# Spreading the rows of w2 unevenly over partitions in a decode kernel

## The chip, the cores and the metric

The kernel runs on one core of one Trainium2 chip. The metric is device time in microseconds, from the start of the launch to its end. A profiled execution gives, beside its own time, a span: the stretch from the first to the last recorded instruction.

The engines are written as in the profile: PE multiplies matrices (PEld loads its weights), DVE and ACT work on vectors, POOL runs the set-up and a few small steps, and SP issues nearly all transfers. Transfers run on 16 DMA engines. The profile's times in "us" count from the start of the span.

## The reference

The computation is one decode step: a layer norm, then an attention block over a cache of 65,536 positions in 4 groups of heads, and beside it a mixing MLP; both are added to the input. Cut to what matters:

```python
xn = layernorm(x)                                  # x: 1 x 1 x 1024
# A: attention; 32 query heads share 4 key/value heads, 65536 x 128 each, bf16
q = xn_A @ wq;  p = softmax(q k^T / sqrt(128));  A = (p v) @ wo
# B: mixer
h  = gelu(layernorm(xn) @ w1)                      # w1: 1024 x 1024
hs = concatenate([shift(h[part], step) for four parts]) @ w2   # w2: 1024 x 1024
x1 = xn + hs
B  = x1 + gelu(layernorm(x1) @ w3) @ w4            # w3: 1024 x 3584, w4: 3584 x 1024
out = x + A + B                                    # A takes layernorm(x) as its input
```

The four shifts move `h` along the sequence and pad with zeros. The sequence has one position here, so every shifted part is zero: the vector that multiplies `w2` is all zeros. The kernel holds it as `g_bf`, set to zero by POOL at the start, and still loads `w2` and multiplies with it.

## The kernel before

One large buffer `KV` has three slots of 64 KB on each of the 128 partitions. Everything large passes through it, in this order of issue on SP: `wq` (8 MB, slot 0), `w1` and `w2` (2 MB each, slot 1), `w3` (7 MB, slot 2); then eight pairs of an 8 MB block of keys and an 8 MB block of values, the keys alternately in slots 0 and 2 and the values always in slot 1; then `wo` (8 MB, slot 0) and `w4` in four pieces of 17, 7, 3 and 1 rows per partition (slot 2). Every one of these puts the same number of bytes on every partition. A matrix of R rows lies as R/128 whole rows on each partition (`rows_src`, line 292).

The order of the work is written out by hand. `_op`, `_grp` and `_dma` (lines 117 to 144) record instructions, each with the buffers that it reads and writes, into a list per engine, and a wait is added where another engine has to be done first. SP issues in its order and stops at a wait; so a transfer whose slot is still in use also holds up all that stand behind it. `issue(i)` (line 307) is the load of the i-th key or value block into its slot.

The set-up runs in this order:

- POOL makes constants (lines 315 to 337). It also works inside `layer_norm` (line 355).
- DVE and PE norm `x`, then PE multiplies with `wq` (line 379). When that is done SP may issue the first block of keys into slot 0 (line 384).
- The queries are spread into `Yall` (line 395); a second layer norm follows; then `proj` (line 404) multiplies with `w1`, `gelu` follows, and `proj` multiplies with `w2`. `proj` takes one matrix row per partition at a time: for each of `KT_D` = 8 rows it issues `nt` matmuls of 512 columns (line 411), 2 for `w1` and `w2`, 7 for `w3`; DVE copies the sums (line 419) and PE transposes them (line 426).
- When the matmuls with `w2` are done, SP may issue the first block of values into slot 1 (line 446). A third layer norm, `proj` with `w3` and `gelu` follow, and then SP waits for all engines and issues the second block of keys into slot 2 (lines 450 and 451).

Then comes a loop over the eight blocks (line 594). DVE transposes the keys in place in four pieces (`Ttr`, line 460), PE makes the scores (`QK`, line 474), DVE and ACT the softmax (lines 481 to 502), PE and DVE transpose the weights (lines 505 and 509), and PE multiplies with the values (`PV`, line 518). At the end of a block SP may issue the values of the next block, and behind these the keys of the one after it (lines 633 and 637). In the last block the four pieces of `w4` are issued after the last scores (line 557). At the end PE multiplies with `wo` (line 578) and, as the pieces arrive, with `w4` (line 566); DVE copies the result and SP stores it (lines 647 and 648).

Of the kernel before, what the change touches and what calls it, by code (L numbers as in the profile page):

```python
# [6 lines left out]
BF = mybir.dt.bfloat16  # L7
# [92 lines left out]
def _deps(q, reads, writes):  # L100
    evs = [e for b in reads for e in b.w.items()]
    for b in writes:
        evs += list(b.w.items()) + list(b.r.items())
    q.wait_all(evs, in_order=q.name == "pe")


def _done(ev, reads, writes, partial=False):
    for b in reads:
        b.add_read(ev)
    for b in writes:  # L110
        if partial:
            b.add_write(ev)
        else:
            b.set_write(ev)


def _op(q, fn, reads=(), writes=(), partial=False, loop=False):
    _deps(q, reads, writes)
    ev = q.op(fn, True, loop)
    _done(ev, reads, writes, partial)  # L120
    return ev


def _grp(q, fns, reads=(), writes=(), partial=False):
    _deps(q, reads, writes)
    ev = None
    for i, fn in enumerate(fns):
        ev = q.op(fn, i == len(fns) - 1)
    _done(ev, reads, writes, partial)
    return ev  # L130
# [8 lines left out]
def _dma(q, chan, fn, reads=(), writes=(), partial=False):  # L139
    _deps(q, reads, writes)  # L140
    chan.n += 1
    ev = q.dma(fn, chan.sem, 16 * chan.n)
    _done(ev, reads, writes, partial)
    return ev


def bass_parallel_sum__gqa_block_cached__mixer_s_mlp__decode_kernel(
# [13 lines left out]
    P = 128  # L161
    D = A_x.shape[2]
# [5 lines left out]
    KT_D = D // P  # L168
# [3 lines left out]
    NBLK = HKV * SK // BLK  # L172
    BPH = SK // BLK
    SLOT = BLK * DH // P
    assert DH == P and G == 8 and HKV == 4 and D == 1024 and HQD == 4096 and F == 3584 and SK == 2 * BLK
    SCALE = float(DH) ** -0.5
    EPS = 1e-5

    with ExitStack() as es:
        E = es.enter_context  # L180

        def sb(name, shape, dt):
            return E(nc.sbuf_tensor(name, shape, dt))
# [4 lines left out]
        def sem(name):  # L188
            return E(nc.semaphore(name))
# [25 lines left out]
        sb("pad", [P, pad // 4], F32)  # L215
        KV = sb("KV", [P, 3, SLOT], BF)
        cb_rL = sb("cb_rL", [P, 1], F32)
# [7 lines left out]
        def early(n, dt):  # L225
            size = n * (2 if dt is F32 else 1)
            o = e_off[0]
            e_off[0] = o + (size + 15) // 16 * 16
            assert e_off[0] <= SLOT
            v = KV[:, 2, o:o + size]  # L230
            return v.bitcast(F32) if dt is F32 else v
# [20 lines left out]
        ln_xc = early(KT_D, F32)  # L252
        ln_sq = early(KT_D, F32)
        qT_bf = early(HQ, BF)
        g_bf = early(KT_D, BF)
        h1g_bf = early(KT_D, BF)
        ge_x = early(KT_F, F32)
        ge_a = early(KT_F, F32)
# [11 lines left out]
        q_pool = _Q("pool", sem("c_pool"))  # L270
        q_sp = _Q("sp", None)
        chans = {}

        def chan(name):
            if name not in chans:
                chans[name] = _DmaChan(sem("d_" + name))
            return chans[name]

        b_const = _B()
# [9 lines left out]
        def kv_load(s, ch, src, n, bufs=None):  # L289
            _dma(q_sp, chan(ch), lambda e: e.dma_start(out=KV[:, s, 0:n], in_=src), writes=b_KV[s] if bufs is None else bufs)  # L290

        def rows_src(w, r0, nrow):
            return w.rearrange("(p r) n -> p (r n)", p=P)[:, r0 * w.shape[1]:(r0 + nrow) * w.shape[1]]
# [3 lines left out]
        b_w1 = b_KV[1][0:2]  # L297
        b_w2 = b_KV[1][2:4]
        kv_load(1, "w1", rows_src(B_w1, 0, 8), 8 * D, b_w1)
        _dma(q_sp, chan("w2"), lambda e: e.dma_start(out=KV[:, 1, 8 * D:16 * D], in_=rows_src(B_w2, 0, 8)), writes=b_w2)  # L300
        kv_load(2, "s2", rows_src(B_w3, 0, 8), 8 * F)

        def slot(i):
            m, isv = divmod(i - 3, 2)
            return 1 if isv else 2 * (m % 2)

        def issue(i):
            if i < 3 + 2 * NBLK:
# [3 lines left out]
                src = cache[0, h, nb * BLK:(nb + 1) * BLK, :].rearrange("(p c) d -> p (c d)", p=P)  # L312
                kv_load(slot(i), "v" if isv else "s%d" % slot(i), src, SLOT)

# [6 lines left out]
        def sel(t_, pattern, op, base, mult, fill):  # L321
            return q_pool.op(lambda e: e.affine_select(out=t_, in_=t_, pattern=pattern, compare_op=op, fill=fill, base=base, channel_multiplier=mult))
# [12 lines left out]
        q_pool.wait_all([ev])  # L335
        ev = sel(maskA, [[32, 4], [0, 8]], ALU.is_ge, 31, -1, 0.0)
        b_const.set_write(ev)

        _op(q_dve, lambda e: e.tensor_copy(xT, x_bf), reads=[b_x], writes=[b_xT])  # L339

        def layer_norm(src, b_src, dst_f, dst_bf, b_dst, c0):
# [27 lines left out]
            reads=[b_M, b_misc], writes=[b_misc])  # L369
# [6 lines left out]
        for j in range(KT_D):  # L376
            for b in range(2):
                for jj in range(4):
# [3 lines left out]
                        start=(j == 0), stop=(j == KT_D - 1), tile_position=(0, 32 * jj)))  # L382
# [5 lines left out]
                                                 start=(b + i == 0), stop=True, skip_group_check=True)  # L388
# [4 lines left out]
        for h in range(HKV):  # L393
            for we in range(4):
# [3 lines left out]
                    reads=[b_M, b_const], writes=[b_Y], partial=(h + we > 0))  # L398
# [2 lines left out]

        kvstep = KV[:].ap[0][0]

        def proj(s, o, ncol, vec, bank, reads, c0):
            nper = ncol // P
            nt = nper // 4
            fns = []
            for j in range(KT_D):
                for k in range(nt):
                    mv = bass.AP(KV[:].tensor, s * SLOT + o + j * ncol + 4 * k, [[kvstep, P], [nper, P], [1, 4]])  # L410
                    fns.append(lambda e, j=j, k=k, mv=mv: e.matmul(  # L411
                        S_ps[32 * (k % 4):32 * (k % 4) + 32, bank + k // 4, :], vec[:, j:j + 1].broadcast_to([P, 32]), mv,
                        start=(j == 0), stop=(j == KT_D - 1), tile_position=(0, 32 * (k % 4))))
            nbank = (nt + 3) // 4
            _grp(q_pe, fns, reads=reads, writes=b_S[bank:bank + nbank])
            for b in range(nbank):
                nb = min(4, nt - 4 * b)
                if b == 0:
                    _op(q_dve, lambda e, b=b, nb=nb: e.tensor_copy(pT_f[0:32 * nb, b, :], S_ps[0:32 * nb, bank + b, :]), reads=[b_S[bank + b]], writes=[b_pT[b]])  # L419
                else:  # L420
                    _op(q_act, lambda e, b=b, nb=nb: e.activation(pT_f[0:32 * nb, b, :], S_ps[0:32 * nb, bank + b, :], ACTF.Copy), reads=[b_S[bank + b]], writes=[b_pT[b]])
            fns = []
            for b in range(nbank):
                nb = min(4, nt - 4 * b)
                for c in range(4):
                    fns.append(lambda e, b=b, nb=nb, c=c: e.matmul(  # L426
                        M_ps[:, c0 + 16 * b + c:c0 + 16 * b + 4 * nb:4], pT_f[0:32 * nb, b, c:512:4], ident_f[0:32 * nb, 0:32 * nb:32],
                        start=(b + c == 0), stop=True, skip_group_check=True))
            _grp(q_pe, fns, reads=b_pT[0:nbank] + [b_const], writes=[b_M])

        def gelu(src_ps, width, dst_bf, b_src, b_dst):
# [7 lines left out]
            _op(q_dve, lambda e: e.tensor_tensor(out=dst_bf, in0=a_, in1=xs_, op=ALU.mult), reads=[b_misc], writes=[b_dst])  # L439

        proj(1, 0, D, xn2_bf, 2, b_w1 + [b_xn2], 256)
        gelu(M_ps[:, 256:256 + KT_D], KT_D, h1g_bf, b_M, b_h1)
        proj(1, 8 * D, D, g_bf, 3, b_w2 + [b_const], 272)
        _op(q_dve, lambda e: e.tensor_tensor(out=x1, in0=xn, in1=M_ps[:, 272:272 + KT_D], op=ALU.add), reads=[b_xn, b_M], writes=[b_x1])
        _op(q_dve, lambda e: e.tensor_tensor(out=acc[:], in0=acc[:], in1=M_ps[:, 272:272 + KT_D], op=ALU.add), reads=[b_acc, b_M], writes=[b_acc])
        issue(4)
        layer_norm(x1, b_x1, xn3, xn3_bf, b_xn3, 208)
        proj(2, 0, F, xn3_bf, 0, b_KV[2] + [b_xn3], 288)
        gelu(M_ps[:, 288:288 + KT_F], KT_F, gh_bf[:], b_M, b_gh)
        q_sp.wait_all([(q.sem, q.cnt) for q in (q_pe, q_dve, q_act, q_pool)])  # L450
# [15 lines left out]
        def QK(n):  # L466
# [3 lines left out]
            for we in range(4):  # L470
                w_hi, e_ = divmod(we, 2)
                for cm in range(4):
                    mv = bass.AP(KV[:].tensor, s * SLOT + sub * 8192 + cm * 128 + w_hi * 64 + e_, [[kvstep, P], [512, 16], [2, 32]])
                    fns.append(lambda e, we=we, cm=cm, mv=mv: e.matmul(  # L474
# [119 lines left out]
        for m in range(NBLK):  # L594
            n = 4 * m
# [38 lines left out]
            if m == NBLK - 2:  # L634
                kv_load(0, "wo", A_wo.rearrange("(p r) n -> p (r n)", p=P), SLOT)
            else:
# [93 lines left out]
```

## Time and profile before

| | |
|---|---|
| median of 5 runs | 400.4 us (400.31 to 400.64) |
| profiled execution, its time | 400.39 us |
| its span | 399.1 us |
| bytes read | 169.87 MB |
| busy: DVE | 221.3 us |
| busy: PE | 176.2 us |
| busy: PE weight loads | 60.6 us |
| busy: ACT | 23.9 us |
| busy: POOL | 7.6 us |
| 16 DMA engines, main queue | 98.7% of the span |

The busy times are of engines that work beside each other. The share of the DMA engines is a mean over the 16 of them. Beside instructions the trace keeps two kinds of records of transfers. One is the packets: start, duration and size of each piece that a DMA engine moved, but not the engine's number. The other is the landing marks: the times at which the 16 DMA engines reported their parts of a transfer done, 16 for each transfer.

### The profile page before, as it was taken

The page shows a single profiled execution, that of the slowest core. Times are in us where ns is not written, and L with a number is a line of the kernel's source. Part 1 is how long each engine was busy: PE and PEld are TensorE (multiplying, and loading weights), DVE is VectorE, ACT ScalarE, POOL GpSimd, SP SyncE. Part 2 cuts the span into 40 slices and gives each one's busy share as a digit, 9 for nine tenths or more (in the row PEclk, how much of TensorE's full clock was granted, in tenths as well). Part 3 has the DMA queues.
Part 4 walks back from the last instruction along what each step waited for, and adds up shares of the span by engine and source line. Part 5 has one row for each costly group of instructions (what it writes and reads, how often), then busy time and mean ns, then how long its engine had stood idle before and what let it go on. Part 6 is the DMA issues. An engine that isn't in the chain of part 4 may idle for free.

```text
span 399.1 us, 3500 instructions
## 1 busy us (share of the span) xinstructions
PE 176.2 (44%) x1539; PEld 60.6 (15%) x1539; DVE 221.3 (55%) x260; ACT 23.9 (6%) x50; POOL 7.6 (2%) x31
## 2 busy tenths in 40 slices
PE   0034768148034713570357036413651462147394
PEld 0022335012001200120012011100120110012232
DVE  0024221995298549834984597269647952896200
ACT  1000000011001100110011002000100110011000
POOL 5000000000000000000000000000000000000000
PEclk9998656556755765565558555855585558556979
DMA  9999899999999999999999999999999999999995
GB/s 421 421 388 493 383 434 480 435 420 427 416 440 420 420 461 453 420 427 420 440 427 420 447 466 420 421 420 427 440 427 447 466 420 420 420 427 440 416 414 229
DMA packets 3759, 169.97 MB, mean 426 GB/s; under 512 B 548, under 2 KB 552, under 8 KB 808
## 3 DMA queue, kind: packets, MB, share of 16 engines
q1 hardware_dynamic: 3608, 169.87, 98.7%
q8 instruction: 5, 0.08, 0.1%
q10 hardware_dynamic: 144, 0.00, 0.0%
q14 instruction: 2, 0.02, 0.0%
HBM read 169.87 MB, written 0.00 MB: 426 GB/s over the span
## 4 chain that ended last, share of the span: by engine, by line
DMA 58%; DVE 25%; PE 13%; issue 1%; ACT 1%; SPq 1%; POOL 0%
DMA KV<-in_A_k_cache_dram 45%; DVE KV L460 18%; DMA KV<-in_B_w_dram 8%; DMA KV<-in_A_x_dram 6%; PE S_ps L411 3%; PE OT_ps L518 2%; DVE mrow L481 2%; PE M_ps L426 2%; PE S_ps L474 2%; PE S_ps L379 2%; ACT p_sb L496 1%; DVE Yall L395 1%; DVE pT_f L509 1%; PE PT_ps L505 1%; DVE pT_f L419 1%
## 5 line engine op out<-in xcount | busy, mean ns | idle before, releaser
L460 DVE STREAM_TRANSPOSE KV<-KV 128x4096 f32<-128x4096 f32 x32 | 140.3, 4421 | 43.3 <-DMA KV<-in_A_k_cache_dram 43.3
L474 PE MATMUL S_ps<-KV,Ycur 128*32 128x512 bf16 x512 | 60.7, 623 | 127.2 <-DVE KV L460 127.2
L518 PE MATMUL OT_ps<-KV,pT_f 128*32 128x512 bf16 x512 | 46.3, 501 | 1.2 <-DVE pT_f L509 1.2
L474 PEld LDWEIGHTS S_ps<-KV,Ycur 128*32 128x32 bf16 x512 | 14.3, 126 | 158.9 <-DVE KV L460 141.4
L496 ACT ACTIVATE p_sb<-S_ps,brun 128x1024 bf16<-128x1024 f32 x16 | 17.8, 1113 | 275.1 <-DVE brun L494 174.7
L509 DVE STREAM_TRANSPOSE pT_f<-PT_ps 128x512 f32<-128x512 f32 x32 | 22.5, 702 | 14.0 <-PE PT_ps L505 14.0
L481 DVE TENSOR_REDUCE mrow<-S_ps 128x1 f32<-128x1024 f32 x16 | 19.3, 1205 | 11.3 <-PE S_ps L474 11.3
L484 PE MATMUL M_ps<-Rm,Lmat 128*128 128x16 bf16 x16 | 3.1, 194 | 38.0 <-DVE Rm L482 38.0
L505 PE MATMUL PT_ps<-p_sb,permR 128*128 128x512 bf16 x32 | 18.4, 576 | 0.8
L529 DVE SCALAR_TENSOR_TENSOR O_acc<-O_acc,ff,OT_ps 128x512 f32<-128x512 f32 x12 | 9.0, 748 | 13.9 <-PE OT_ps L518 13.9
L518 PEld LDWEIGHTS OT_ps<-KV,pT_f 128*32 128x32 bf16 x512 | 12.8, 114 | 23.6 <-issue 15.3
L411 PE MATMUL S_ps<-KV 128*32 128x512 bf16 x88 | 12.6, 564 | 2.7 <-DVE KV L359 2.7
L339 DVE CAST KV<-KV 128x8 f32<-128x8 bf16 x1 | 0.2, 172 | 22.1 <-DMA KV<-in_A_x_dram 22.1
L578 PE MATMUL S_ps<-KV,o_bf 128*1 128x512 bf16 x64 | 9.3, 463 | 5.1 <-DMA KV<-in_A_wo_dram 5.1
L484 PEld LDWEIGHTS M_ps<-Rm,Lmat 128*128 128x128 bf16 x16 | 1.7, 104 | 49.3 <-DVE Rm L482 49.3
L426 PE MATMUL M_ps<-ident_f,pT_f 64*128 64x2 f32 (+2 forms) x32 | 7.9, 372 | 2.4 <-DVE pT_f L419 2.4
L582 DVE COPY pT_f<-S_ps 1x512 f32<-1x512 f32 x1 | 0.7, 680 | 14.4 <-PE S_ps L578 14.4
L426 PEld LDWEIGHTS M_ps<-ident_f,pT_f 64*128 64x128 f32 (+2 forms) x32 | 7.7, 326 | 4.7 <-DVE pT_f L419 3.4
L419 DVE COPY pT_f<-S_ps 64x512 f32<-64x512 f32 (+1 forms) x3 | 2.1, 686 | 11.3 <-PE S_ps L411 11.3
L505 PEld LDWEIGHTS PT_ps<-p_sb,permR 128*128 128x128 bf16 x32 | 3.3, 103 | 26.9 <-ACT p_sb L496 14.7
L364 PE MATMUL M_ps<-KV 8*128 8x8 bf16 x1 | 0.2, 181 | 15.9 <-DVE Dmat_f L363 15.9
L379 PE MATMUL S_ps<-KV 128*32 128x512 bf16 x64 | 6.2, 572 | 1.4 <-DVE KV L359 1.4
(88 smaller groups left out, 87.4 us busy)
## 6 DMA issues: line engine op xcount, KB each, us to landing
KV<-in_B_w_dram SPq DMA_DIRECT2D x1, 7168.0 KB, 47.9
KV<-in_B_w_dram SPq DMA_DIRECT2D x1, 4352.0 KB, 27.4
KV<-in_B_w_dram SPq DMA_DIRECT2D x2, 2048.0 KB, 28.1
KV<-in_B_w_dram SPq DMA_DIRECT2D x1, 1792.0 KB, 31.4
KV<-in_B_w_dram SPq DMA_DIRECT2D x1, 768.0 KB, 32.7
KV<-in_B_w_dram SPq DMA_DIRECT2D x1, 256.0 KB, 32.9
KV<-in_A_k_cache_dram SPq DMA_DIRECT2D x8, 46.7
KV<-in_A_v_cache_dram SPq DMA_DIRECT2D x8, 27.8
```

The lines of the kernel that those rows point to most:

```text
L379: fns.append(lambda e, j=j, b=b, jj=jj: e.matmul(S_ps[32 * jj:32 * jj + 32, b, :], xn_bf[:, j:j + 1].broadcast_to([P, 32]), KV[:, 0, j * H ...
L411: fns.append(lambda e, j=j, k=k, mv=mv: e.matmul(S_ps[32 * (k % 4):32 * (k % 4) + 32, bank + k // 4, :], vec[:, j:j + 1].broadcast_to([P, ...
L426: fns.append(lambda e, b=b, nb=nb, c=c: e.matmul(M_ps[:, c0 + 16 * b + c:c0 + 16 * b + 4 * nb:4], pT_f[0:32 * nb, b, c:512:4], ident_f[0:3 ...
L460: _op(q_dve, lambda e: e.transpose(out=KV32[:, s, o:o + 4096], in_=KV32[:, s, o:o + 4096]), reads=[b_KV[s][sub]], writes=[b_KV[s][sub]], l ...
L474: fns.append(lambda e, we=we, cm=cm, mv=mv: e.matmul(S_ps[32 * cm:32 * cm + 32, n % 4, :], Ycur[:, we, :, :].rearrange("p a g -> p (a g)") ...
L481: _op(q_dve, lambda e: e.reduce_max(mrow[:, k:k + 1], S_ps[:, 2 * k:2 * k + 2, :].rearrange("p b c -> p (b c)"), axis=AX.X), reads=b_S[2 * ...
L496: _op(q_act, lambda e: e.activation(p_sb[:, :, :].rearrange("p b c -> p (b c)"), S_ps[:, 2 * k:2 * k + 2, :].rearrange("p b c -> p (b c)") ...
L505: _op(q_pe, lambda e: e.matmul(PT_ps[:, :], permR[:, :], p_sb[:, n % 2, :], start=True, stop=True), reads=[b_p[n % 2], b_const], writes=[b ...
L509: _op(q_dve, lambda e: e.transpose(out=pT_f[:, n % 2, :], in_=PT_ps[:, :]), reads=[b_PT], writes=[b_pT[n % 2]], loop=True)
L518: fns.append(lambda e, q=q, q4=q4: e.matmul(OT_ps[32 * q4:32 * q4 + 32, g % 2, :], pT_bf[:, n % 2, q, :, 1], KV[:, s, 8192 * sub + 512 * q ...
L529: _op(q_dve, lambda e: e.scalar_tensor_tensor(out=O_acc[:, 0:512], in0=O_acc[:, 0:512], scalar=ff[:, k:k + 1], in1=OT_ps[:, k, :], op0=ALU ...
L578: _grp(q_pe, [lambda e, j=j, jj=jj: e.matmul(S_ps[32 * jj:32 * jj + 1, 1, :], o_bf[:, j:j + 1], KV[:, 0, j * D + 512 * jj:j * D + 512 * (j ...
```

## The change

`w2` has 1024 rows, 8 on each partition before. After the change its rows lie in three groups, in slot 1 behind `w1`:

- 7 rows on each of the 128 partitions (896 rows), one transfer, in the place in SP's order where `w2` stood;
- 5 rows on each of 16 partitions, numbers 32, 36, ... 92 (80 rows), one transfer;
- 2 rows on each of 24 partitions (48 rows), in eight transfers of three partitions each: 0, 4, 8; 1, 5, 9; and so on to 35, 39, 43.

The second and third group are issued by SP behind `w3`. As they fill only some partitions, POOL first sets their place to zero on all partitions (7 rows, 7168 elements), behind its other constants, and SP waits for that. `proj` gets a parameter for the number of rows: for `w2` it is 14 instead of 8, so it issues 28 matmuls instead of 16, and these wait for all ten transfers. `g_bf` has 14 columns instead of 8, all zero as before.

```diff
+    NA, NS, NB = 7, 5, 2
...
-        g_bf = early(KT_D, BF)
+        g_bf = early(NA + NS + NB, BF)
...
-        _dma(q_sp, chan("w2"), lambda e: e.dma_start(out=KV[:, 1, 8 * D:16 * D], in_=rows_src(B_w2, 0, 8)), writes=b_w2)
+        ROWS = P * NA
+        o_s = 8 * D + NA * D
+        o_b = o_s + NS * D
+        b_w2s = _B()
+        b_w2b = [_B() for _ in range(8)]
+        _dma(q_sp, chan("w2"), lambda e: e.dma_start(out=KV[:, 1, 8 * D:8 * D + NA * D], in_=B_w2[0:ROWS, :].rearrange("(p r) n -> p (r n)", p=P)), writes=b_w2)
         kv_load(2, "s2", rows_src(B_w3, 0, 8), 8 * F)
+
+        def w2_rest():
+            _op(q_pool, lambda e: e.memset(KV[:, 1, o_s:o_b + NB * D], 0.0), writes=[b_w2s] + b_w2b)
+            _dma(q_sp, chan("w2s"), lambda e: e.dma_start(out=KV[32:96:4, 1, o_s:o_b], in_=B_w2[ROWS:ROWS + 16 * NS, :].rearrange("(p r) n -> p (r n)", p=16)), writes=[b_w2s])
+            for i in range(8):
+                p0 = 32 * (i // 4) + i % 4
+                r0 = ROWS + 16 * NS + 3 * NB * i
+                _dma(q_sp, chan("w2b"), lambda e, p0=p0, r0=r0: e.dma_start(out=KV[p0:p0 + 12:4, 1, o_b:o_b + NB * D], in_=B_w2[r0:r0 + 3 * NB, :].rearrange("(p r) n -> p (r n)", p=3)), writes=[b_w2b[i]])
...
         b_const.set_write(ev)
+        w2_rest()
...
-        def proj(s, o, ncol, vec, bank, reads, c0):
+        def proj(s, o, ncol, vec, bank, reads, c0, nrow=KT_D):
...
-            for j in range(KT_D):
+            for j in range(nrow):
...
-                        start=(j == 0), stop=(j == KT_D - 1), tile_position=(0, 32 * (k % 4))))
+                        start=(j == 0), stop=(j == nrow - 1), tile_position=(0, 32 * (k % 4))))
...
-        proj(1, 8 * D, D, g_bf, 3, b_w2 + [b_const], 272)
+        proj(1, 8 * D, D, g_bf, 3, b_w2 + [b_w2s] + b_w2b + [b_const], 272, NA + NS + NB)
```

More of the change, by code (lines that the diff above doesn't have):

```diff
@@ L299, in bass_parallel_sum__gqa_block_cached__mixer_s_mlp__decode_kernel @@
         kv_load(1, "w1", rows_src(B_w1, 0, 8), 8 * D, b_w1)
-        _dma(q_sp, chan("w2"), lambda e: e.dma_start(out=KV[:, 1, 8 * D:16 * D], in_=rows_src(B_w2, 0, 8)), writes=b_w2)
-        kv_load(2, "s2", rows_src(B_w3, 0, 8), 8 * F)
+        ROWS = P * NA
+        o_s = 8 * D + NA * D
+        o_b = o_s + NS * D
+        assert ROWS + 16 * NS + 24 * NB == D and o_b + NB * D <= SLOT
+        b_w2s = _B()
+        b_w2b = [_B() for _ in range(8)]
+        _dma(q_sp, chan("w2"), lambda e: e.dma_start(out=KV[:, 1, 8 * D:8 * D + NA * D], in_=B_w2[0:ROWS, :].rearrange("(p r) n -> p (r n)", p=P)), writes=b_w2)
+        kv_load(2, "s2", rows_src(B_w3, 0, 8), 8 * F)
+        def w2_rest():
[5 more added lines that the diff above has]
+                _dma(q_sp, chan("w2b"), lambda e, p0=p0, r0=r0: e.dma_start(out=KV[p0:p0 + 12:4, 1, o_b:o_b + NB * D], in_=B_w2[r0:r0 + 3 * NB, :].rearrange("(p r) n -> p (r n)", p=3)), writes=[b_w2b[i]])
         def slot(i):
```

## The prediction

> **What bounds the kernel now.** The page's slices and queues come first: is any engine busy all the time?
>
> ```profile
> DMA  9999899999999999999999999999999999999995
> ...
> DMA packets 3759, 169.97 MB, mean 426 GB/s; under 512 B 548, under 2 KB 552, under 8 KB 808
> ...
> q1 hardware_dynamic: 3608, 169.87, 98.7%
> q8 instruction: 5, 0.08, 0.1%
> ...
> q14 instruction: 2, 0.02, 0.0%
> ...
> DMA 58%; DVE 25%; PE 13%; issue 1%; ACT 1%; SPq 1%; POOL 0%
> ```
>
> The 16 DMA engines are busy in every slice but the last; no other engine is. The chain's 58% is too low a measure, because it walks through compute while transfers run beside it. The list of waits and then the timeline of the end show who sets the time (in the timeline: start, length, and in brackets the idle time before and who ended it):
>
> ```profile
> DVE KV L460 <- DMA KV<-in_A_k_cache_dram: 43.3, 7, 8.4
> ```
>
> ```profile
> 394.08 0.94 PE L566 MATMUL S_ps<-KV,gh_bf 128*1 128x256 bf16 x28 [1.26 <-DMA KV<-in_B_w_dram]
> 395.94 0.93 PE L566 MATMUL S_ps<-KV,gh_bf 128*1 128x256 bf16 x16 [0.93 <-DMA KV<-in_B_w_dram]
> 396.92 0.42 DVE L647 CAST orow<-S_ps 128x256 bf16<-128x256 f32 x1 [7.34 <-PE S_ps L566]
> 397.37 0.62 SPq L648 DMA_DIRECT2D out_dram<-orow  x1
> ```
>
> Each block of keys is waited for, and so is each late piece of w4. The end is the landing of the last piece of w4, at 396.53 us by its last landing mark, plus 2.5 us to the span's end.
>
> A mean over 16 engines hides which one is late, so I follow the packet records. An engine's packets lie end to start (64 KB in 2.418 us, next start some 6 ns later), and this gives sixteen chains, numbered here 0 to 15 by their first packet. None has a gap from 1.8 us to the end. Their marks for the last piece of w4 split: ten at 394.52 to 394.92 us, six at 396.01 to 396.53 us. Five of the six fell behind one by one. The page's five q8 packets (16 KB of instructions each, at 45.86, 79.40, 103.35, 142.30 and 393.78 us, 1.02 to 1.09 us long) and two of q14 each set one chain back by 0.3 to 1.5 us: chain 13 (46 us), 5 (55 us), 3 (79 us), 4 (103 us), 8 (142 us), 5 again (259 us). Chain 5 is last of all: its part of the third w4 piece ends at 395.41 us, against 394.86 to 395.15 us on 3, 4, 8 and 13. Chains 0 to 2 are among the early ten. So the time is the load of chain 5, and bytes moved from it to chains 0 to 2 are worth their own transfer time, up to the 1.5 us between the groups.
>
> **The change part by part.** The sum is made against the profiled execution, 400.39 us (span 399.1); the median is 400.4, the same.
>
> *Bytes on thirteen chains.* w2 goes from 8 rows to 7 on each of the 8 partitions of an engine, plus 5 rows on one. From w1's end to w2's end a chain takes 4.86 us now (eight packets of 16 KB). Eight of 14 KB take 4.30 us (the second w4 piece), saving 0.56. The 10 KB packet lies between the 6 KB row (0.234 us: third w4 piece, 1.87 us for eight) and the 14 KB row (0.537): 0.386, with its 4-byte semaphore packet 0.40. Net -0.16 us on chains 3 to 15.
>
> *Bytes on three chains.* Eight packets of 4 KB more. The 2 KB packets of the last piece take some 0.08 us each, the 6 KB ones 0.234: 0.158, plus 0.015 for a semaphore packet of each transfer: 1.38. Net +1.22 us on chains 0 to 2. Their marks move from at most 394.92 to at most 396.14 us, still ahead of chain 5 at 396.53 - 0.16 = 396.37.
>
> *Price of nine small transfers.* No row shows a transfer to 3 partitions. From below it is bytes alone: 26 KB at 64 KB in 2.418 us, +0.98 instead of +1.22. From above, let each cost what the whole 256 KB last piece costs behind its neighbour, 0.64 us from mark to mark (395.89 to 396.53): 9 x 0.64 = 5.8, net +5.2 us on chains 0 to 2, an end at 400.1 and 404.0 us in all. I take the packets: the last piece, also queued behind others, runs at 0.08 us a packet with no gap.
>
> The Trainium skill speaks against this part. DMA: Bandwidth & Descriptors, in its rules for kernel authors, says to merge small transfers, those under 64 KB being mostly overhead; each of the eight is 24 KB. Its fit of about 2 us fixed per transfer (section on the anatomy of one DMA) is for another issuing path; nine of them paid in a row would be 18 us, and an estimated 412 us, by that page. The w4 rows contradict it for transfers that queue: 256 KB landed 0.64 us after its neighbour.
>
> *POOL's memset and SP's wait.* A memset of 64x512 f32 takes 0.52 us here, one of 128x128 bf16 0.20; 7168 elements are then between 7168/512 x 0.52 = 7.3 us and half of it. POOL's set-up ends at 6.6 us, so the memset ends by 14 us. Behind it on POOL stands only the pow of the first layer norm, which waits for x until 26.28 us. Behind SP's wait stand nine issues of 0.33 to 0.70 us, then the first key block, issued at 33.59. All done by 21 us: covered, costs nothing; without the cover it would delay that block, whose bytes the rings need at about 47 us.
>
> *The product with w2.* This moves. The chain of the span's end has now, with start and length first:
>
> ```profile
> 42.59 3.62 PE S_ps L411 x16
> ...
> 49.00 2.96 PE S_ps L411 x16
> 51.98 0.69 DVE pT_f L419
> ```
>
> PE is ready at 48.93, when w2 has long landed (31.7 us). After the change the small parts arrive behind w3. Chains 0 to 2 end w3 at 47.84 - 0.56, then take 0.40 + 1.38: 49.06, and with 0.45 us from a chain's end to its mark 49.5. Chain 13, set back at 46 us, has 49.53 - 0.56 + 0.40 + 0.45 = 49.8. So PE waits 0.9 us. Behind it on PE stand the w2 transposes and the third layer norm. Then 14 rows instead of 8: weight loads show 0.4275 us a row at half clock (43.00, 43.43, 43.85), 3.62 + 6 x 0.4275 = 6.19 us, ending at 56.0 instead of 51.97. Delay D = 4.0 us. Bounds: 2.2 (no wait, faster clock, 2.96 x 14/8) and 7.7 (small transfers at the 5.8 above).
>
> D runs on to the first values (issue 51.97 to 56.0; the key block in transit lasts to 67 us, covered), the second keys (70.92 to 74.9; the values last to 86 us, covered), the first transposes and block 0's end. Next late is an issue of SP (the SP timeline):
>
> ```profile
> 70.92 0.33 SPq L290 DMA_DIRECT2D KV<-in_A_k_cache_dram  x1
> 100.45 0.33 SPq L290 DMA_DIRECT2D KV<-in_A_v_cache_dram  x1
> 100.82 0.44 SPq L290 DMA_DIRECT2D KV<-in_A_k_cache_dram  x1
> 138.14 0.33 SPq L290 DMA_DIRECT2D KV<-in_A_v_cache_dram  x1
> ```
>
> The second values go out at 100.45 + 4.0 = 104.5. From issue to first packet is 1.21 us (the store at the end: 397.37 to 398.58), so data flows at 105.7. Among the thirteen, the chains that run dry first end the second keys at 106.00 - 0.16 = 105.84: 0.2 us of slack. Chain 5 ends them at 106.90 - 0.16 = 106.74: 1.1 us. So no chain waits. If the early ones do, they have over a microsecond to lose; they matter only near 396.4. The nearest is chain 8, set back later, at 142 us: about 396.2 now, 0.3 us behind what it may lose. Block 1's transposes start at the keys' landing as before, and DVE, done with block 0 at 105.4, is free.
>
> *More instructions.* PE gains 12 matmuls and 12 weight loads, SP nine issues, POOL one. They lie in the cover above.
>
> Sum: -0.16 us at the end, 400.39 - 0.16 = 400.23. About 0.2% (0.8 us) is what a measurement of this kernel tells from no change, so this is the same time.
>
> **The rivals.** *The small transfers hit a late engine (slower).* The chains carry no numbers in the trace; that the first three are the engines that serve these 24 partitions is my assumption, from the order in which the first packets start. If chain 5 were among them: 400.39 + 1.22 = 401.6. Were all 24 partitions on one early chain, 48 rows are 96 KB, 3.6 us: 394.92 - 0.16 + 3.6 = 398.4, so 402.2. For it: no row of a 3-partition transfer. Against: the first starts rise from 1.015 to 1.81 us in even steps, like one pass over sixteen rings.
>
> The Trainium skill has a rule on it that no run here shows: the page above, in its section on the semaphore's 16, lets a transfer use as many engines as divide its slowest dimension, at most 16, the lowest-numbered ones; that gives engines 0 to 2, and the end the sum has.
>
> *The second values come late (slower).* Past D = 5.1 chain 5 itself runs dry, and each further microsecond counts in full; past 6.1 it is slower by 0.8 us. With D at its bound 7.7: 7.7 - 5.1 - 0.16, 402.8. For it: 0.2 us of slack on the early chains. Against: only a wait of 3 us for w2's parts, where 0.9 is worked out, gets there.
>
> *One more fetch of instructions (slower).* If the longer program brings a fetch onto a chain of the late group, that chain loses 1.0 to 1.5 us: 401.2 to 401.7. For it: seven fetches, six on late chains. Against: some 34 instructions more beside 3500.
>
> The Trainium skill (Runtime: NRT & Kernel Launch, instruction fetch mechanics) states blocks of 16 KiB, 256 instructions; the q8 packets agree with the size.
>
> *Faster.* A fetch that moves off chain 5 uncovers the next late chain, 0.27 us ahead; 399.9. Over 0.2% needs several to move.
>
> **How the numbers follow.** Forecast 0.70. Wrong engine 0.07, late values 0.08, one more fetch 0.09, faster 0.06. Of the late values 0.03 and of the faster case 0.03 stay within 0.2%, so same 0.76, slower 0.21, faster 0.03. The range runs from 399.9 (the spread of the five runs, 0.33 us, below the forecast, which is also the faster case) to 401.6 (wrong engine, most of the extra fetch); late values beyond it and the small transfers at their upper bound are left out, less than 2 in 10.
>
> **What would show it.** In the changed kernel: the second product with 28 matmuls starting near 49.8 and the first values issued near 56.0; the second values near 104.5; no gap in the DMA slices near 106 us; keys landing 0.1 to 0.2 us earlier per block; the last w4 wait ending near 396.4. A gap after 104 us, the small parts landing past 52 us, or more than five q8 packets would prove it wrong.

## The result, and the profile after

The changed kernel takes 400.69 us (median of 27 runs, 400.03 to 402.40), the kernel before, beside it, 400.44 (49 runs, 400.23 to 401.09). The ratio is 1.0016, with a 95% interval of 1.0009 to 1.0023: a little slower, where the forecast was 0.16 us faster.

The runs say more than the median. They fall into two groups with a gap between: 15 runs from 400.03 to 400.91 us (median 400.34) and 12 from 401.37 to 402.40. The kernel before has no second group; its highest of 49 is 401.09. Below they are called the lower and the upper group. So the change costs nothing in some executions and 0.9 to 2.0 us in others, and the question is what differs between them.

The profiled execution of the changed kernel, 400.39 us, is one of the lower group. Its page, slices and queues:

```profile
span 399.1 us, 3535 instructions
...
DMA  9989999999999999999999999999999999999995
...
DMA packets 3839, 169.97 MB, mean 426 GB/s; under 512 B 588, under 2 KB 592, under 8 KB 872
...
q1 hardware_dynamic: 3688, 169.87, 98.8%
q8 instruction: 5, 0.08, 0.1%
...
q14 instruction: 2, 0.02, 0.0%
```

The bytes are the same, the packets 80 more, the fetches of instructions (q8, q14) as many as before. The timeline of the end, and the issues of SP that the forecast speaks of (start, length):

```profile
394.09 0.94 PE L582 MATMUL S_ps<-KV,gh_bf 128*1 128x256 bf16 x28 [1.83 <-DMA KV<-in_B_w_dram]
...
396.95 0.42 DVE L663 CAST orow<-S_ps 128x256 bf16<-128x256 f32 x1 [7.93 <-PE S_ps L582]
397.40 0.60 SPq L664 DMA_DIRECT2D out_dram<-orow  x1
```

```profile
12.61 0.61 SPq L312 DMA_DIRECT2D KV<-in_B_w_dram  x1
13.26 5.66 SPq L316 DMA_DIRECT2D KV<-in_B_w_dram  x8
33.49 0.35 SPq L291 DMA_DIRECT2D KV<-in_A_k_cache_dram  x1
54.66 0.33 SPq L291 DMA_DIRECT2D KV<-in_A_v_cache_dram  x1
73.63 0.33 SPq L291 DMA_DIRECT2D KV<-in_A_k_cache_dram  x1
103.38 0.33 SPq L291 DMA_DIRECT2D KV<-in_A_v_cache_dram  x1
```

The nine small issues end at 18.9 us, under cover. A transfer to three partitions has landing marks of three DMA engines, not of 16, and one more at its issue. The last mark of w4 is at 396.57 us, against 396.54 before. The second values go out at 103.38 instead of 100.45 us: the delay D is 2.9 us in this execution. The product with w2 that makes it, from the timeline:

```profile
50.02 4.62 PE L427 MATMUL S_ps<-KV 128*32 128x512 bf16 x28 [1.13 <-DMA KV<-in_B_w_dram]
```

It starts near the forecast time (49.8) but takes 4.62 us, not 6.19. The clock granted to PE is 0.70 of full speed over the product, 50.02 to 54.64 us, and 0.76 from 49.96 to 55.97; the forecast took half.

Near 106 us some DMA engines now do wait, which the prediction had named as a sign against it. To weigh that I add up, over the 16 engines and from 104.5 to 110 us, the time in which an engine has no packet of data and the time by which the 64 KB packets that start in this stretch exceed 2.418 us. A fetch of instructions that falls into this stretch alone makes some 1.5 us of it. In the kernel before the sum is 0.1 us, in this execution 6.7, a mean of 0.3 per engine beyond the fetch. It falls on engines that are early anyway: on average over the 16 engines the second values land 0.33 us later than in the kernel before, the last of them at the same time (127.42 us in both), and so it costs nothing at the end.

### The profile page after: what moved, and what is told of

It is laid out like the page before. It is cut to its first block, busy times and chain, and to the rows that moved or that the text cites. A ratio compares the mean times of both kernels' runs of the same rounds, so it can differ in the third digit from the quotient of the medians.

```text
span 399.1 us, 3535 instructions
## 1 busy us (share of the span) xinstructions
PE 179.5 (45%) x1551; PEld 62.5 (16%) x1551; DVE 221.3 (55%) x260; ACT 23.9 (6%) x50; POOL 13.7 (3%) x32
## 4 chain that ended last, share of the span: by engine, by line
DMA 61%; DVE 23%; PE 10%; POOL 3%; ACT 1%; issue 1%; SPq 1%; POOLq 0%
DMA KV<-in_A_k_cache_dram 44%; DMA KV<-in_B_w_dram 18%; DVE KV L476 18%; PE S_ps L427 3%; PE OT_ps L534 2%; DVE mrow L497 2%; PE S_ps L490 2%; POOL KV L311 2%; PE M_ps L442 1%; ACT p_sb L512 1%; DVE pT_f L525 1%; POOL KV L337 1%; PE PT_ps L521 1%; DVE O_acc L545 0%; DVE pT_f L435 0%
## 5 line engine op out<-in xcount | busy, mean ns | idle before, releaser
L534 PE MATMUL OT_ps<-KV,pT_f 128*32 128x512 bf16 x512 | 47.2, 509 | 1.2 <-DVE pT_f L525 1.2
L534 PEld LDWEIGHTS OT_ps<-KV,pT_f 128*32 128x32 bf16 x512 | 13.0, 115 | 23.8 <-issue 15.9
L427 PE MATMUL S_ps<-KV 128*32 128x512 bf16 x100 | 14.6, 566 | 3.8 <-DVE KV L375 2.7
```

The costliest lines, as they stand in the source:

```text
L427: fns.append(lambda e, j=j, k=k, mv=mv: e.matmul(S_ps[32 * (k % 4):32 * (k % 4) + 32, bank + k // 4, :], vec[:, j:j + 1].broadcast_to([P, ...
L534: fns.append(lambda e, q=q, q4=q4: e.matmul(OT_ps[32 * q4:32 * q4 + 32, g % 2, :], pT_bf[:, n % 2, q, :, 1], KV[:, s, 8192 * sub + 512 * q ...
```

## The experiments

The theory is that the delay on the path through the product with w2 makes the second values late: "late second values", a rival in the prediction. Against it stand the small transfers by themselves, and fetches of instructions that hit a late engine. Each kernel was timed beside the kernel before on the same chip. The last two ran once each, for their profile, on another chip than the other experiments; the kernel before took 400.87 us in its one run there.

**The change's transfers without the long product.** Edit to the changed kernel (inside `proj` the row in memory is `j % nmem`):

```diff
-        proj(1, 8 * D, D, g_bf, 3, b_w2 + [b_w2s] + b_w2b + [b_const], 272, NA + NS + NB)
+        proj(1, 8 * D, D, g_bf, 3, b_w2 + [b_const], 272, 8, NA)
...
+        _deps(q_sp, [b_w2s] + b_w2b, [])
         issue(4)
```

> The changed kernel with all its transfers, but the product with w2 takes 8 rows (16 matmuls, the first row of seven again as the eighth) and waits only for the 7-row transfer; SP waits for the small transfers before the first values. This leaves the small rows of w2 out of the product. Theory 'late second values': the delay D is gone, the second values go out near 100.4 us, no DMA engine runs dry near 106 us, and the time is 400.1 to 400.4 in every run, with none above 401. Rival 'small transfers or instruction fetches cost a late engine': nothing changes for them, so runs of 401.4 to 402.4 stay, in about two of five as in the changed kernel.

Measured: 400.33 us (11 runs, 400.17 to 400.61) against 400.52 for the kernel before, ratio 0.9997 (0.9988 to 1.0006). No run is above 400.61. All ten transfers are there, and the upper group is gone. The second values go out at 100.82 us:

```profile
100.82 0.33 SPq L291 DMA_DIRECT2D KV<-in_A_v_cache_dram  x1
```

**The long product without the change's transfers.** Edit to the kernel before (rows 0 to 5 are used a second time):

```diff
-        proj(1, 8 * D, D, g_bf, 3, b_w2 + [b_const], 272)
+        proj(1, 8 * D, D, g_bf, 3, b_w2 + b_KV[2] + [b_const], 272, 14)
```

> The kernel before with its equal transfers, but the product with w2 has 14 rows (28 matmuls, rows 0 to 5 a second time) and waits for w3's landing, so it starts near 50 us. Theory 'late second values': the delay alone makes the changed kernel's times, a group near 400.4 and a group near 401.5 to 402.5. Rival 'small transfers': the bytes are as before, so every run is 400.3 to 400.8.

Measured: 400.68 us (11 runs, 400.14 to 402.38), ratio 1.0010 (1.0000 to 1.0020). Seven runs are from 400.14 to 400.80, four from 401.31 to 402.38: the two groups of the changed kernel, with the equal transfers of the kernel before. Its profile is of one from the upper group, 402.37 us. Product, issue of the second values and end, from its timeline:

```profile
49.99 5.96 PE L411 MATMUL S_ps<-KV 128*32 128x512 bf16 x28 [1.53 <-DMA KV<-in_B_w_dram]
```

```profile
104.59 0.33 SPq L290 DMA_DIRECT2D KV<-in_A_v_cache_dram  x1
...
399.41 0.62 SPq L648 DMA_DIRECT2D out_dram<-orow  x1
```

Here the product takes 5.96 us, the values go out 1.2 us later than in the changed kernel's first profile, and the store of the result 2.0 us later. The loss near 106 us is 15.9 us over the 16 engines. Not all of the delay is from there: the last landing mark of the second values is 1.14 us later than in the kernel before, that of the third keys 2.31, while the mean over the 16 marks hardly moves (0.87 and 0.90). In between, the fetch of instructions at 139.95 us fell on one engine that was late already.

**A longer product still**, in the kernel of the last edit:

```diff
-        proj(1, 8 * D, D, g_bf, 3, b_w2 + b_KV[2] + [b_const], 272, 14)
+        proj(1, 8 * D, D, g_bf, 3, b_w2 + b_KV[2] + [b_const], 272, 24)
```

> As the run before it, with 24 rows (48 matmuls), which puts the second values out some 3 to 4.3 us later again, near 107 to 108 us. Theory 'late second values': every DMA engine runs dry at the end of the second keys, and every run is slower, by 2 to 4 us (402.4 to 404.4). Rival 'small transfers': 400.3 to 400.8, no effect of a delay off the DMA engines' path.

Measured: 402.40 us (5 runs, 401.84 to 402.57), ratio 1.0045 (1.0031 to 1.0059). Every time lies above 401.8. The product took 7.19 us, less than the ten rows more would give at half clock; the second values went out at 106.06 us, a little before the expected 107, and the 1.9 us over the kernel before lie just below the expected 2 to 4. The loss near 106 us is 23.8 us over the engines.

```profile
106.06 0.33 SPq L290 DMA_DIRECT2D KV<-in_A_v_cache_dram  x1
```

The marks of the second values now lie within 0.4 us of each other: no engine is early any more. The last of them is only 0.34 us later than in the kernel before; the rest of the delay comes after it, when a fetch at 139.16 us, on whichever engine it falls, makes a latest engine (the last mark of the third keys is 1.54 us later), and from slower packets around 180 us, told of at the end.

**The small transfers ahead of w3.** Edit to the changed kernel: the line that issues w3 moves.

```diff
-        kv_load(2, "s2", rows_src(B_w3, 0, 8), 8 * F)
...
         w2_rest()
+        kv_load(2, "s2", rows_src(B_w3, 0, 8), 8 * F)
```

> The changed kernel with its nine small transfers issued ahead of w3 instead of behind it: PE no longer waits for them at 48.9 us, the 14 rows stay. Theory 'late second values': D falls by 1.1 us from the changed kernel's 2.9 to 4, the second values go out near 102.5 to 103.3, and most runs of the slow group vanish: 400.1 to 400.6 in nine of ten. Rival 'small transfers': same bytes and packets, so the slow group stays at about two of five.

Measured: 400.20 us (11 runs, 400.00 to 400.62) against 400.52, ratio 0.9996 (0.9986 to 1.0005). None of the 11 lies above 400.62. The product starts at 48.66 us, the second values go out at 103.04, and the loss near 106 us is 2.1 us over the engines, little more than the fetch in that stretch.

```profile
103.04 0.33 SPq L291 DMA_DIRECT2D KV<-in_A_v_cache_dram  x1
```

**The change with DVE work moved off the path.** Edit: the 16 steps that write `Yall` stand behind the first `gelu`, and the norm's scratch column is 330 instead of 204, so that the sums that `Yall` reads stay intact.

```diff
-        for h in range(HKV):
-            for we in range(4):
-                _op(q_dve, lambda e, h=h, we=we: e.tensor_tensor(out=Yall[:, h, we, :, :],
...
-        layer_norm(xn, b_xn, xn2, xn2_bf, b_xn2, 204)
+        layer_norm(xn, b_xn, xn2, xn2_bf, b_xn2, 330)
...
         gelu(M_ps[:, 256:256 + KT_D], KT_D, h1g_bf, b_M, b_h1)
+        for h in range(HKV):
+            for we in range(4):
+                _op(q_dve, lambda e, h=h, we=we: e.tensor_tensor(out=Yall[:, h, we, :, :],
...
```

> The changed kernel, whole, with one move: the 16 DVE steps that write Yall (3.6 us) stand behind the first gelu, where DVE waits for the product with w2, instead of ahead of the second layer norm. All transfers, rows and waits of the change stay. Theory 'late second values': PE reaches the product with w2 earlier but must wait for its small transfers to 49.9 us, so the product starts as in the changed kernel and the move saves nothing: D stays 2.9 to 4, and the slow group (401.3 to 402.4) stays. If the group vanishes although the second values still go out after 103.3 us, the theory is wrong. Rival 'instruction fetches': the slow group stays as well.

Measured: 402.28 us (6 runs: 400.45, and five from 401.77 to 403.07), ratio 1.0054 (1.0041 to 1.0068). As expected, the move saves nothing as long as the last of the nine small transfers lands at 49.8 us: in the profiled execution, 400.45 us, PE waits 4.87 us for them instead of 1.13 and the values go out at 103.76. The upper group did stay, and became the usual one: five of six runs instead of 12 of 27, with times up to 403.07 us. That was not expected, and why is left open below.

**Both moves together**, the two edits above:

> The small transfers ahead of w3 and the 16 DVE steps of Yall behind the first gelu: neither the wait nor the DVE steps stand before the product with w2, which can start near 45.2 us. Theory 'late second values': the second values go out near 100 us, before or at the time of the kernel before, so no engine runs dry and no run is above 400.7; the median is 400.2 to 400.3, by the 0.16 us of bytes. Rival 'small transfers': 401.3 to 402.4 in two of five.

Measured: 400.18 us (11 runs, 399.99 to 400.59) against 400.45, ratio 0.9994 (0.9985 to 1.0003). The product starts at 43.51 us (45.2 was expected), the second values go out at 99.79, and the loss near 106 us is 0.0. This is the best version tried; its interval still holds no change.

**The same move on the kernel before**, as a control:

> The kernel before with the 16 DVE steps of Yall behind the first gelu, nothing else. The product with w2 starts near 45.3 instead of 48.9 us and the second values go out near 97. Theory 'DMA engines set the time': 400.3 to 400.6, the same as before, since no engine ran dry there. If a delay on this path counts at all in the kernel before, it is faster by some tenths of a us.

Measured: 400.47 us (11 runs, 400.36 to 400.67) against 400.45, ratio 1.0001 (0.9992 to 1.0010). The product starts at 45.32 us, as expected, but the second values go out at 99.75, not near 97: DVE now waits 0.67 us for the first block of keys, and starts on it at 69.56 us, where it started at 70.91. In the kernel before the path has room, and earlier is worth nothing.

**More bytes on the three engines.** Edit to the version with both moves:

```diff
-    NA, NS, NB = 7, 5, 2
+    NA, NS, NB = 6, 4, 8
```

> As the run with the tail first and the DVE steps later, with the rows split 6 on every partition, 4 on 16 partitions and 8 on the 24: 13 DMA engines get 52 rows each and three get 116. Theory 'the latest DMA engine sets the time, by its bytes': the three gain -0.79 + 8 x 0.62 = 4.2 us on the kernel before, end at 399.1 and set the time, 402.9 to 403.1. Rival 'the end is set by compute or by the slots coming free': 400.2 to 400.6.

Measured: 402.54 us (5 runs, 402.45 to 402.64) against 400.45, ratio 1.0053 (1.0039 to 1.0066): 2.1 us more, where 2.5 to 2.6 were expected. Its last wait is for w4, by the timeline:

```profile
398.24 0.92 PE L582 MATMUL S_ps<-KV,gh_bf 128*1 128x256 bf16 x16 [0.97 <-DMA KV<-in_B_w_dram]
399.22 0.42 DVE L663 CAST orow<-S_ps 128x256 bf16<-128x256 f32 x1 [7.92 <-PE S_ps L582]
```

Three engines have become the late ones: their last marks of w4 are at 398.47 to 398.84 us, all others at 396.72 or earlier. A late engine does set the time by its bytes.

**Two more profiles**, of the changed kernel and of the change with DVE's steps moved, in the hope of the upper group:

> The changed kernel once more, for a profile of one of its slow executions (two of five were above 401.3). Theory 'late second values': if this execution is above 401.3, the product with w2 takes more than the 4.62 us of the profile at hand (up to 6.2, by PE's clock), the second values go out past 104 us, and the DMA engine that ends last is one that lost time near 106 us or was hit by a fetch of instructions after that. If it is near 400.4, they go out before 104 us.

> The changed kernel with the DVE steps of Yall later, which had five of six runs above 401.7, for a profile of a slow one: second values out past 103.8 us, marks of the second values spread up to 128 to 128.6 us instead of 127.4 to 127.8, and the last mark of w4 at 398 or later. If the second values go out by 103.8 and the run is still above 401.3, something else slows it.

Measured: 401.71 and 401.82 us, both in the range of the upper group, and 0.84 and 0.95 us above the kernel before on that chip. The changed kernel at 401.71 us, its product, the clock in the same stretch of both its profiles (length; busy times; the granted clock is the number ahead of the DMA share), and its issue and end:

```profile
49.96 5.98 PE L427 MATMUL S_ps<-KV 128*32 128x512 bf16 x28 [1.51 <-DMA KV<-in_B_w_dram]
```

```profile
49.96:55.97 6.01, 5.98 (x28) 2.16 (x28) 0.00 (x0) 0.00 (x0) 0.00 (x0) 0.53 1.09 470
```

```profile
49.96:55.97 6.01, 5.18 (x31) 2.38 (x31) 1.02 (x3) 0.00 (x0) 0.00 (x0) 0.76 1.09 470
```

```profile
55.97 0.33 SPq L291 DMA_DIRECT2D KV<-in_A_v_cache_dram  x1
74.23 0.33 SPq L291 DMA_DIRECT2D KV<-in_A_k_cache_dram  x1
104.61 0.33 SPq L291 DMA_DIRECT2D KV<-in_A_v_cache_dram  x1
...
398.71 0.60 SPq L664 DMA_DIRECT2D out_dram<-orow  x1
```

The first windows line is of the execution of 401.71 us, the second of that of 400.39 us. The same 28 matmuls start at the same time; at 0.53 of the clock they take 5.98 us, at 0.70 over the matmuls themselves they take 4.62. The second values go out at 104.61 instead of 103.38, and the result is stored 1.3 us later (398.71 to 397.40).

The product is not the whole of these 1.23 us. At the second keys the difference is 0.60 (74.23 to 73.63); from 56 to 73 us the clock was the higher one in the slower execution, 0.79 against 0.71. The other 0.63 us arise at the end of block 0, in the last matmuls ahead of the issue. The clock there, again first the execution of 401.71 us, then that of 400.39:

```profile
100.00:104.00 4.00, 4.00 (x45) 1.26 (x41) 1.80 (x4) 0.00 (x0) 0.00 (x0) 0.57 1.06 459
```

```profile
100.00:104.00 4.00, 3.15 (x45) 0.78 (x33) 1.90 (x4) 0.00 (x0) 0.00 (x0) 0.93 1.06 459
```

The landing marks show where the time is lost. Against the kernel before, the last mark is 0.17 us earlier at the second keys, 1.62 us later at the second values, and 1.34 us later at the last piece of w4; the means over the 16 engines are 0.02, 0.96 and 0.97 us later. So what the end has lost was lost between 106 and 129 us. In the execution of 401.82 us most of it is lost there too: the last mark is 1.29 us later at the second values and 1.46 at the end.

The number of instruction packets is the same in both:

```profile
q8 instruction: 5, 0.08, 0.1%
...
q14 instruction: 2, 0.02, 0.0%
```

The profiles of all kernels whose engines carry the bytes of the kernel before or of the change, by the issue of the second values; the last column is the sum over 16 engines described above:

| kernel | second values out | its time | loss near 106 us |
|---|---|---|---|
| before, DVE later | 99.75 | 400.42 | 0.0 |
| both moves | 99.79 | 400.18 | 0.0 |
| before | 100.45 | 400.39 | 0.1 |
| short product | 100.82 | 400.50 | 1.5 |
| small transfers first | 103.04 | 400.47 | 2.1 |
| changed, lower group | 103.38 | 400.39 | 6.7 |
| changed, DVE later, lower group | 103.76 | 400.45 | 8.3 |
| before, long product | 104.59 | 402.37 | 15.9 |
| changed, upper group | 104.61 | 401.71 | 18.5 |
| changed, DVE later, upper group | 104.88 | 401.82 | 12.6 |
| before, longer product | 106.06 | 402.57 | 23.8 |

Up to 103.04 us hardly anything is lost but the fetch. To 103.8 engines lose time, but the last mark of w4 comes at most 0.14 us later than in the kernel before; past 104.5 it comes 1.3 to 2.2 us later.

## Why the prediction was wrong

- *What bounds the kernel* was right. The end is the last piece of w4 on the latest DMA engine, as the run with 6, 4 and 8 rows shows.
- *Bytes on three chains* was right in size: three engines carry the 4 KB packets, one every 0.160 us with its semaphore packet (0.173 worked out). That these are the first three chains was assumed, and does not hold. In the changed kernel's profile, followed back packet by packet, at least two of the three began at 1.044 us or later, where the first three chains began at 1.005 to 1.028. By luck it did no harm: the sum holds for any three early engines, and none of the three is the one that the fetch at 45 us set back. *The small transfers hit a late engine* is not what makes the upper group: three versions with all these transfers (the short product, the small transfers first, both moves) have no run above 400.62 us, and the long product without them has the group.
- *Price of nine small transfers*: the packets' price held. The eight landed by 49.66 us and the transfer to 16 partitions by 49.88, on the engine hit by the fetch at 45 us; 49.5 and 49.8 were forecast. Each of the eight carries 12 KB, three packets of 4 KB, not the 24 KB of the prediction. The 412 us there is where the last mark would come by the page; the time would be near 416. The rule of the Trainium skill against small transfers (DMA: Bandwidth & Descriptors, rules for kernel authors) is not what cost time: the kernel with all nine and a short product has no upper group.
- *Bytes on thirteen chains*: a 10 KB packet took 0.385 to 0.391 us, as worked out, but -0.16 us is smaller than one profile can show. The first marks of the engines differ by some 0.2 us between executions, and the last mark of w4 was 0.03 us later, not 0.16 earlier. Over the runs the three versions without late values have medians 0.19, 0.32 and 0.27 us below the kernel before, the sign of the forecast; each one's interval includes no change.
- *One more fetch of instructions* is refuted: five and two packets in every profile. Which engine a fetch falls on does matter where late values have left no engine early, as in the long and the longer product.
- *The product with w2*: D = 4.0 us was near for the upper group (104.61 - 100.45 = 4.16) and too long for the lower one (2.93). The forecast took PE at half clock throughout the product, which is one of two cases. That D is the same at the second values is in part luck: it is 4.00 us at the first values (55.97 - 51.97), 3.31 at the second keys and 4.16 at the second values.
- *The step that failed is the slack behind D.* The prediction put "0.2 us of slack" on the chains that run dry first and 1.1 us on chain 5, from 1.21 us between an issue and its first packet, and concluded "So no chain waits". That 1.21 us is from the store at the end, which finds idle engines and moves 2 KB. For 8 MB behind a transfer that is still running, the time from issue to first packet differs from engine to engine and can be three times as long. With the issue at 104.61 us (401.71 us) the first packets begin 1.1 to 3.7 us after it. Two of them begin at 108.19 and 108.30 us, although the last engine had ended the second keys at 107.46: two engines wait at least 0.7 us, however late they were. With the issue at 103.38 us four engines wait, up to 0.8 us, and begin 2.8 to 3.3 us after it. At 103.04 us, 2.5 us ahead of the first engine's end at 105.53, hardly any engine waits. And the first packets are slow, on engines that waited and on engines that did not: with the issue at 104.61 us they take mostly 2.9 to 3.5 us, the next ones 2.6 to 2.9, instead of 2.42. So D = 4.0 lay beyond the slack, and the rival *the second values come late*, priced from D = 5.1 on and given 0.08, is what decides, from somewhere between D = 3.3 (103.76 us, no loss at the end) and 4.1 (104.59).
- The first row of this very profile gave a warning: the first 64 KB packets of the kernel, which find engines at rest, begin 1.0 to 1.8 us after their issue and take 2.69 to 3.45 us.

## What to carry to other kernels

A transfer queue that never runs dry has a lead, and a change that delays the compute which frees the next buffer spends it. Take that lead from transfers of the same size under the same load, engine by engine, and count the longer first packets; here an issue 2.5 us ahead of the first engine's end was early enough and one 2.0 us ahead was not quite, where an idle store showed 1.2. A gain of tenths in bytes is lost easily if a longer product lies on the path to the next issue, and the loss is avoided by giving that path its room back, here by issuing the small pieces ahead of the large one.

## What was not expected of the hardware

One and the same kernel met two courses of PE's granted clock: over the product it was 0.70 in the changed kernel's profile of 400.39 us and 0.53 in that of 401.71, a difference of 1.36 us for 28 matmuls, and from 100 to 104 us 0.93 and 0.57. That this divides all 27 runs into the two groups is inferred from these two profiles, and the long product's at 402.37 us (0.53 over its product) fits it. In the kernel before the clock changes too (0.50 from 49.96 to 55.97 us, 1.00 from 100 to 104), but its second values go out 2.6 us ahead of the latest issue at which hardly anything was lost (100.45 and 103.04). What decides the phase of the clock in an execution stays open.

A fetch costs a busy engine more than its packet lasts: the 8 KB one at 259 us, 0.33 us long, set its engine back by 0.97 us, in the kernel before and in the changed one. The prediction named chain 5 for this; chains 5 and 6 began in the same nanosecond, 1.122 us, and it may have been 6.

In the kernel with 24 rows the 64 KB packets took 2.49 us on average from 170 to 200 us, against 2.42 elsewhere, while all engines landed within 0.5 us of each other but the one hit by the fetch at 139 us; in the execution of 401.82 us they took 2.45. Why they took longer there was not tried, and neither was why the change with DVE's steps moved falls into the upper group more often (five of six) than the change alone (12 of 27).
